# One core, RWKV-5 attention followed by a Wave-MLP block: the same tasks in another hand-written order on every engine, with other choices of engine, PSUM bank, load order and filler matmuls

## The chip, the cores and the metric

The kernel runs on one core of a Trainium2 chip. The metric is device time in microseconds (us), the median of several runs; lower is better. A core has five engines that run at the same time, each through its own list of instructions, strictly in order: PE (matrix multiply; "PEld" is its loading of weights), DVE (vector), ACT (scalar, with lookup functions), POOL (general purpose) and SP (which here only starts DMA transfers). An instruction that waits for another engine or for a transfer holds up everything behind it on its own engine. PE writes only to PSUM, of which there are eight banks; DVE and ACT read them out.

## The reference

Inputs are r, k, v of shape (4, 8, 768, 48), a decay w and a bonus u per head and channel, and four weight matrices. Two stages follow each other, the first one's output y being the second one's input x (4 x 768 x 384).

```python
for t in range(S):                       # attention, for each batch and head
    y[t] = r[t] @ (state + outer(u * k[t], v[t]))
    state = w[:, None] * state + outer(k[t], v[t])

theta = x @ w_theta                      # Wave-MLP
zr, zi = x * cos(theta), x * sin(theta)
u_ = x + w_tok_r @ zr + w_tok_i @ zi     # mixes the 768 tokens of a batch
out = u_ + relu(u_ @ w_ch)
```

## The kernel before

The recurrence is done in chunks. The work is cut into 12 groups of 256 tokens: batch b has groups 3b, 3b+1 and 3b+2. Within a group the decays are folded into r and k (tiles `Rw`, `Kw`, line 563 or 565: load times a table of powers), both are turned on PE (`flip`, L499, into PSUM) and copied out (`RT`, `KT`, L514 on ACT or L515 on DVE). PE multiplies them into scores (L606 or L619), DVE multiplies the scores by a causal mask (`mAT`, L631), and PE adds mask times v (L786, L852), states times r (L773, L827) and a diagonal bonus (L802) into a bank that becomes the attention output `x` (L810, L812, L862). The state runs from group to group: PE forms outer products of `Kw` and v (L689), DVE adds them up (`F`, `T`, L724), `N` is the decayed state that the next group starts from, and `Sb`, `Sd` are its bf16 copies. `PD` (L642) and `yd` (L668) serve the bonus. v is cast to bf16 as `vb` (L584 on ACT, L586 on DVE, L588 on POOL).

Then `x` is turned (into `xT`), PE multiplies by w_theta (L876), ACT takes cosine and sine (L883, L887), and DVE forms `z` (L891), which holds x cos and x sin. When all three groups of a batch have their z, PE mixes the tokens: 6 output tiles of 128 tokens, each in three parts of four matmuls (L912, one part for each group's z), 72 parts in all. DVE adds x (`un`, in the tile `uu_all`, L930), the result is turned (`uT`, in `uu_all` too), PE multiplies by w_ch (L944), and DVE or ACT and POOL finish the output (`fin_all`, L953, L950, L957), which SP writes out, 256 tokens at a time (L968) and for the last group 128 at a time (L963). A turn is done on PE with a copy, or by a DMA transpose that SP starts (L505); both ends are then in SBUF.

The weights come in through transfers that POOL issues (L468), land in buffers that other tiles use later (`z`, `x`, `uu_all`, `fin_all`), and are turned on PE into `WrT` and `WiT`. They may start only when k and r of group 0 have landed (the list `gate`).

`Plan.add` records 777 tasks with what each reads and writes; it works out which earlier tasks each must wait for. Nothing is scheduled by rule: six tables decide. `ORDER` is the order in which the tasks are issued, and so the order on each engine; `WAYS` picks, task by task, one of the task's possible engines; `BANKS` gives each PSUM use its bank; `AFTER` holds pairs (a, b): b also waits for a; `IDLE` holds (task, bank, n): n matmuls whose result nobody reads ("unread", from `zero`, L289) are issued right behind a task; `WARM` are 6 and 8 more such matmuls that are tasks of their own. The unread matmuls keep PE active where it would wait. The tasks below are named by what they write and the number of the group: `Kw0` in a row of the order is the buffer 0 of `Kw`.

Of the kernel before, what the change touches and what calls it, by code (L numbers as in the profile page):

```python
# [93 lines left out]
)  # L94

AFTER = [
    (84, 77), (87, 130), (170, 136), (492, 604),
]

IDLE = [  # L100
    (5, 0, 3), (30, 2, 4), (118, 5, 1), (116, 2, 2), (85, 3, 2), (88, 6, 2),
]


# [907 lines left out]
```

## Time and profile before

| | us |
|---|---|
| median of 3 runs | 140.81 (140.75 to 141.16) |
| the profiled execution, its own time | 140.54 |
| its span, from the first to the last instruction | 138.8 |
| PE busy | 127.3 (92%) |
| DVE busy | 112.2 (81%) |
| ACT busy | 79.0 (57%) |
| POOL busy | 48.9 (35%) |

The mean granted TensorE clock of the execution is 0.995. A group of instructions is named by line, engine and operation; "x8" is a count; the square bracket in a row of the timeline is how long the engine stood idle just before and whose work ended that. Matmuls overlap, so a single matmul's duration is longer than the distance to the next; the chain of waits gives the distance. The span is 1.74 us shorter than the execution's time, and the execution is 0.27 us faster than the median.

### The profile page before, as it was taken

To read this page: it belongs to the slowest core of one execution; us is meant where nothing else is said; L and a number is where in the kernel's file an instruction comes from. 1 tells how busy PE (TensorE), PEld (TensorE's weight loads), DVE (VectorE), ACT (ScalarE), POOL (GpSimd) and SP (SyncE) were. 2 spreads that over 40 slices of the span, in tenths; PEclk is the share of its full clock that TensorE was granted. 3 is DMA by queue.
4 is the path that set the end of the run, shared out by engine and by line. 5 is a ranking of instruction groups with operands and counts; after the bars stand their busy time and mean duration, and the time that the engine had idled before them with its cause. 6 is when DMAs were issued, how large, how long until landed. Compare 5 with 4: busy or idle time off the path is not lost.

```text
span 138.8 us, 5143 instructions
## 1 busy us (share of the span) xinstructions
PE 127.3 (92%) x2217; PEld 84.3 (61%) x2217; DVE 112.2 (81%) x218; ACT 79.0 (57%) x153; POOL 48.9 (35%) x57
## 2 busy tenths in 40 slices
PE   7959997989999997999999999988999999999980
PEld 2345664756678855768666676855666666655630
DVE  7599978867689999999999899994979779446480
ACT  4479897497428995899768743555910150550100
POOL 8006677490000790799000019926054311000000
PEclk9999999999999999999999999999999999999997
DMA  3999999999989980328999983999900636740545
GB/s 95 324 325 290 201 213 210 222 239 249 261 234 305 250 183 4 114 82 224 214 226 268 192 178 69 122 143 302 231 5 6 112 64 137 219 159 0 113 158 182
DMA packets 64021, 24.72 MB, mean 178 GB/s; under 512 B 58621, under 2 KB 63998, under 8 KB 63998
## 3 DMA queue, kind: packets, MB, share of 16 engines
q1 hardware_dynamic: 61520, 21.44, 65.9%
q0 software_dynamic: 2464, 2.95, 12.2%
q8 instruction: 17, 0.28, 0.9%
q14 instruction: 6, 0.05, 0.1%
q10 hardware_dynamic: 14, 0.00, 0.0%
HBM read 20.06 MB, written 4.72 MB: 179 GB/s over the span
## 4 chain that ended last, share of the span: by engine, by line
PE 66%; DVE 13%; ACT 9%; issue 5%; DMA 4%; ACTq 0%; DVEq 0%
PE bank L912 31%; PE bank L876 7%; PE bank L499 7%; PE bank L944 6%; PE bank L289 4%; DMA uu_all<-uu_all 4%; DVE mAT L631 4%; ACT KT L514 2%; PE bank L689 2%; ACT RT L514 2%; PE bank L852 2%; DVE fin_all L953 2%; PE bank L786 1%; PE bank L619 1%; PE bank L827 1%
## 5 line engine op out<-in xcount | busy, mean ns | idle before, releaser
L912 PE MATMUL bank<-z,WrT 128*128 128x384 bf16 x144 | 46.9, 326 | 0.5 <-ACT WrT L514 0.5
L912 PE MATMUL bank<-z,WiT 128*128 128x384 bf16 x144 | 46.8, 326 | 0.0
L642 POOL TENSOR_TENSOR PD<-RT,KT 128x1024 bf16<-128x1024 bf16 x4 | 8.5, 2126 | 33.6 <-ACT RT L514 31.9
L631 DVE TENSOR_TENSOR mAT<-bank,mask 128x512 bf16<-128x512 f32 x28 | 18.1, 682 | 1.4 <-PE bank L606 1.2
L912 PEld LDWEIGHTS <-WiT 128*128 128x128 bf16 x144 | 14.1, 98 | 8.4 <-issue 0.6
L912 PEld LDWEIGHTS <-WrT 128*128 128x128 bf16 x144 | 14.1, 98 | 8.4 <-DVE z L891 0.3
L887 ACT ACTIVATE trig<-bank 128x384 f16<-128x384 f32 x24 | 11.5, 494 | 11.5 <-PE bank L876 11.5
L930 DVE TENSOR_TENSOR uu_all<-bank,x 128x384 bf16<-128x384 f32 x24 | 13.1, 552 | 5.5 <-PE bank L912 5.0
L944 PE MATMUL bank<-Wch,uu_all 128*128 128x384 bf16 x72 | 15.0, 327 | 1.5 <-DMA uu_all<-uu_all 1.1
L953 DVE SCALAR_TENSOR_TENSOR fin_all<-bank,uu_all 128x384 f32<-128x384 f32 x23 | 12.1, 552 | 4.5 <-PE bank L944 4.2
L891 DVE TENSOR_TENSOR z<-x,trig 128x1536 bf16<-128x1536 bf16 x12 | 12.1, 1016 | 3.8 <-ACT trig L883 2.4
L883 ACT ACTIVATE trig<-bank,pi 128x384 f16<-128x384 f32 x24 | 13.3, 580 | 2.8 <-PE bank L876 2.8
L876 PE MATMUL bank<-Wth,xT 128*128 128x384 bf16 x72 | 14.5, 326 | 0.0
L668 POOL TENSOR_TENSOR yd<-dg,vb 128x768 bf16<-128x768 f32 x7 | 10.3, 1472 | 11.2 <-DVE z L891 5.1
L514 ACT ACTIVATE RT<-bank 128x1024 bf16<-128x1024 bf16 x12 | 12.3, 1026 | 0.3 <-PE bank L499 0.3
L514 ACT ACTIVATE KT<-bank 128x1024 bf16<-128x1024 bf16 x10 | 10.3, 1028 | 2.6 <-PE bank L499 2.6
L289 PE MATMUL bank<-zero 128*128 128x512 bf16 x28 | 8.8, 446 | 1.2 <-DVE zero L296 1.0
L944 PEld LDWEIGHTS <-uu_all 128*128 128x128 bf16 x72 | 6.2, 97 | 5.9 <-DMA uu_all<-uu_all 1.8
L563 DVE TENSOR_TENSOR Rw<-ld,rpow 128x768 bf16<-128x768 f32 x9 | 9.7, 1089 | 0.0
L499 PE MATMUL bank<-ident,Rw 128*128 128x128 bf16 x96 | 7.3, 219 | 1.7 <-DVE Rw L563 1.4
L876 PEld LDWEIGHTS <-xT 128*128 128x128 bf16 x72 | 6.5, 98 | 3.7
L499 PE MATMUL bank<-ident,Kw 128*128 128x128 bf16 x96 | 7.2, 219 | 1.4 <-DVE Kw L563 1.4
(121 smaller groups left out, 222.3 us busy)
## 6 DMA issues: line engine op xcount, KB each, us to landing
ld<-in_r_dram SPq DMA_DIRECT2D x12, 384.0 KB, 5.0
out_dram<-fin_all SPq DMA_DIRECT2D x11, 384.0 KB, 3.0
ld<-in_k_dram SPq DMA_DIRECT2D x7, 384.0 KB, 6.5
ld<-in_v_dram SPq DMA_DIRECT2D x7, 384.0 KB, 5.3
ld<-in_v_dram SPq DMA_DIRECT2D x10, 192.0 KB, 3.7
ld<-in_k_dram SPq DMA_DIRECT2D x10, 192.0 KB, 3.8
uu_all<-in_moe_w_tok_r_dram POOLq DMA_DIRECT2D x1, 384.0 KB, 7.1
z<-in_moe_w_tok_i_dram POOLq DMA_DIRECT2D x1, 384.0 KB, 8.6
```

Source lines behind the costliest of these rows:

```text
L289: ins = [nc.tensor.matmul(bank_t[k][:, :wide * C].rearrange("p (a c) -> p a c", a=wide), zero, bc(zero, 1, wide), start=True, stop=True, s ...
L499: ins = [nc.tensor.matmul(bank16(tok)[:, i * C:(i + 1) * C], s, ident, is_transpose=True, start=(i == 0), stop=(i == n - 1)) for i, s in e ...
L514: ways = [act(n * C, lambda: nc.scalar.activation(dst, src(), Act.Copy)), dve(n * C, lambda: nc.vector.tensor_copy(dst, src()), 1.0 if pai ...
L631: mask01[:, j] if pairs else mask_c): nc.vector.tensor_mul(
L876: ins = [nc.tensor.matmul(bank(th)[:, :HD], xT[:, t, dk, :], Wth[:, dk, :], start=(dk == 0), stop=(dk == ND - 1)) for dk in range(ND)]
L883: P.add(act(HD, lambda th=th, t=t, trig=trig: nc.scalar.activation(trig[:, t, 0], bank(th)[:, :HD], Act.Sin, bias=pi2), 144), use=[th], rd ...
L887: P.add(act(HD, lambda th=th, t=t, trig=trig: nc.scalar.activation(trig[:, t, 1], bank(th)[:, :HD], Act.Sin)), use=[th], rd=["sin"], wr=[( ...
L891: P.add(dve(4 * HD, lambda trig=trig, pr=pr: nc.vector.tensor_mul(z[:, 2 * pr:2 * pr + 2], bc(x[:, 2 * pr:2 * pr + 2], 2, 2), trig), 2.0, ...
L912: ins.append(nc.tensor.matmul(bank(tm)[:, :HD], (WrT, WiT)[ri][:, so, to * C:(to + 1) * C], z[:, so, ri], start=(part == 0 and i == 0), st ...
L930: P.add(dve(HD, lambda tm=tm, t=t, to=to, un=un: nc.vector.tensor_add(un[:, t], bank(tm)[:, :HD], x[:, to])), use=[tm], rd=[("x", xi, pr, ...
L944: ins = [nc.tensor.matmul(bank(tf)[:, :HD], uT[:, t, dk, :], Wch[:, dk, :], start=(dk == 0), stop=(dk == ND - 1)) for dk in range(ND)]
L953: nc.vector.scalar_tensor_tensor(fin[:, t], bank(tf)[:, :HD], 0.0, un[:, t], op0=Alu.max, op1=Alu.add))], use=[tf], rd=[("un", j, t)],
```

## The change

`ORDER`, `WAYS`, `BANKS`, `AFTER` and `IDLE` are replaced; the code is otherwise the same and computes the same values. Each engine's list is thereby another, from the first rows to the last. Over the whole program these counts change, among others: decays (`Rw`, `Kw`) on DVE 17 to 11, on POOL 7 to 13; `PD` on DVE 8 to 10, on POOL 4 to 2; `yd` on DVE 5 to 3, on POOL 7 to 9; turns of `x` by DMA 5 to 7, of `un` by DMA 8 to 7; unread matmuls 28 to 26. The first line of `ORDER` and the two short tables in the diff:

```diff
-    1, 8, 37, 0, 15, 7, 19, 5, 2, 9, 28, 36, 29, 16, 11, 112, 6, 18, 14, 12, 10, 20, 17, 21,
...
+    1, 18, 38, 2, 15, 0, 28, 5, 112, 7, 37, 19, 9, 6, 8, 16, 11, 10, 29, 20, 154, 21, 36, 77,
...
 AFTER = [
-    (84, 77), (87, 130), (170, 136), (492, 604),
+    (157, 90), (84, 158), (127, 87), (432, 434), (645, 653),
 ]
 
 IDLE = [
-    (5, 0, 3), (30, 2, 4), (118, 5, 1), (116, 2, 2), (85, 3, 2), (88, 6, 2),
+    (30, 2, 5), (118, 4, 2), (88, 7, 3), (116, 2, 1), (96, 1, 1),
 ]
```

Task 5 is the warm-up of 8 unread matmuls, task 4 the one of 6, 30 the turn of w and u ("wu flip"). Task 4 stood far behind 30, between the scores of group 1 and the outer products of group 1; it now stands right ahead of 30. Task 90 is a POOL copy of a state that now waits for `Kw` of group 2 on DVE; 158 is a POOL `Rw` that waits for `PD` on DVE; 87 is `yd` of group 0, now on POOL, waiting for `PD` of group 1; 434 is an `N` on POOL that waits for a DVE copy.

Three places of the lists follow. First DVE at the start, from the first decay on; before:

```order
L563 TENSOR_TENSOR Kw0_108<-ld0_90,kpow_81 128x8x2x48
L563 TENSOR_TENSOR Rw0_106<-ld1_91,rpow_80 128x8x2x48
L563 TENSOR_TENSOR Rw1_107<-ld4_94,rpow_80 128x8x2x48
L563 TENSOR_TENSOR Kw1_109<-ld3_93,kpow_81 128x8x2x48
L642 TENSOR_TENSOR PD0_125<-RT0_118,KT0_122 128x1024
L435 TENSOR_TENSOR uw_89<-bank1_62,wup_86 64x4 x2
L631 TENSOR_TENSOR mAT0_127<-bank6_67,mask01_72 128x512
L631 TENSOR_TENSOR mAT0_127<-bank5_66,mask01_72 128x512
L563 TENSOR_TENSOR Kw2_110<-ld6_96,kpow_81 128x8x2x48
```

and now:

```order
L563 TENSOR_TENSOR Rw0_106<-ld1_91,rpow_80 128x8x2x48
L303 MEMSET pi2_76 128x1
L563 TENSOR_TENSOR Rw1_107<-ld4_94,rpow_80 128x8x2x48
L563 TENSOR_TENSOR Kw0_108<-ld0_90,kpow_81 128x8x2x48
L563 TENSOR_TENSOR Kw1_109<-ld3_93,kpow_81 128x8x2x48
L563 TENSOR_TENSOR Kw2_110<-ld6_96,kpow_81 128x8x2x48
L420 COPY wup_86<-bank1_62 128x4
L435 TENSOR_TENSOR uw_89<-bank1_62,wup_86 64x4 x2
L724 TENSOR_TENSOR T0_136<-bank6_67,F0_131 128x192
L642 TENSOR_TENSOR PD0_125<-RT0_118,KT0_122 128x1024
L631 TENSOR_TENSOR mAT0_127<-bank0_61,mask01_72 128x512
```

All five decays come first, k's behind r's; on SP the load of k for group 0 (`ld0`) goes from second to fifth place, behind v (`ld2`), r of group 1, r of group 0 and k of group 2. Second, POOL from the `Kw` of group 3 on; before:

```order
L563 TENSOR_TENSOR Kw3_111<-ld9_99,kpow_81 128x8x2x48
L468 DMA Wch_172<-in_moe_w_ch_dram 128x3x384
L642 TENSOR_TENSOR PD0_125<-RT0_118,KT1_123 128x1024
L668 TENSOR_TENSOR yd0_157<-dg0_154,vb3_115 128x768
L752 TENSOR_TENSOR N0_134<-T1_137,w256_87 128x192
L563 TENSOR_TENSOR Rw1_107<-ld0_90,rpow_80 128x8x2x48
```

and now:

```order
L563 TENSOR_TENSOR Kw3_111<-ld9_99,kpow_81 128x8x2x48
L712 CAST Sd3_153<-N1_135 64x4x48
L468 DMA x2_162<-in_moe_w_tok_i_dram 128x2x768
L468 DMA z1_164<-in_moe_w_tok_r_dram 128x2x768
L563 TENSOR_TENSOR Kw0_108<-ld12_102,kpow_81 128x8x2x48
L468 DMA Wch_172<-in_moe_w_ch_dram 128x3x384
L563 TENSOR_TENSOR Kw2_110<-ld2_92,kpow_81 128x8x2x48
L563 TENSOR_TENSOR Rw0_106<-ld3_93,rpow_80 128x8x2x48
L712 CAST Sd1_151<-F2_133 64x4x48
L668 TENSOR_TENSOR yd0_157<-dg0_154,vb3_115 128x768
L752 TENSOR_TENSOR N0_134<-T1_137,w256_87 128x192
L565 TENSOR_TENSOR Kw3_111<-ld5_95,kpow_c_82 128x16x48
```

Between the first decay and the next `yd` there are now three more decays. Third, SP at the end, which starts the last transfers; before:

```order
L505 DMA_TRANSPOSE xT1_168<-x0_160 128x6x128
L968 DMA out_0_dram<-fin_all_169 128x2x384 x2
L505 DMA_TRANSPOSE uu_all_170<-uu_all_170 128x6x128 x2
L968 DMA out_0_dram<-fin_all_169 128x2x384 x2
L963 DMA out_0_dram<-fin_all_169 128x384 x2
```

and now:

```order
L505 DMA_TRANSPOSE xT1_168<-x0_160 128x6x128
L968 DMA out_0_dram<-fin_all_169 128x2x384
L505 DMA_TRANSPOSE uu_all_170<-uu_all_170 128x6x128
L968 DMA out_0_dram<-fin_all_169 128x2x384
L963 DMA out_0_dram<-fin_all_169 128x384 x2
L968 DMA out_0_dram<-fin_all_169 128x2x384
```

The last output is now one of 256 tokens (group 9), and one of the last two turns of `un` by DMA is gone: it stands on PE, at the end of its list.

More of the change, by code (lines that the diff above doesn't have):

```diff
@@ new lines @@
+    "000001000100000000100000000000100010000000000000000000012000000000000000010110110000"
+    "000000101101100000000001011011000011000020000000000000000100000112000000000000110000"
+    "000001002010200100000000120000000000000100000000000000100000000012000000000000000120"
+    "110110000000001201100000000000012011011000000100000001001001010000100000000120000000"
+    "000000100000010000010000000000000001200000000000011000100000000201000000000120000000"
+    "000000001201101100000000012011011000000000120110000000000000101101100000000012011011"
@@ L88 @@
+    "000000000000110000110"
 )
 BANKS = (
-    "001234567234675130425576152715460374061573605146037162051426713475123045341605273015"
-    "634562104315704367413076250376245013720167023146506560560312652405712436150274652367"
-    "5103450617406471260754161352613507413062130630714523"
+    "001123456720451670123546126452317416032413472051307510473062072307320536502615643746"
+    "172304637125036471506451726501362456731450371265140104023574602471062354731524713062"
+    "745164305721643271506153402714026174325061064327150"
```

13 lines of the change are left out of this document (3 added, 10 removed), and 82 rows, old and new, of the table ORDER.

## The prediction

> **What bounds the kernel now.** I read the page's busy shares and slices first, then a table by stretches of 10 us, then the timelines of PE, DVE and POOL where PE had gaps, and last the end of the chain of waits. The page's first part and its chain by engine:
>
> ```profile
> PE 127.3 (92%) x2217; PEld 84.3 (61%) x2217; DVE 112.2 (81%) x218; ACT 79.0 (57%) x153; POOL 48.9 (35%) x57
> PE 66%; DVE 13%; ACT 9%; issue 5%; DMA 4%; ACTq 0%; DVEq 0%
> ```
>
> PE is the bound, and a reorder does not change what PE must do; it can only change the 138.8 - 127.3 = 11.5 us in which PE stands idle. Where those lie, from the table by stretches (us; busy time of PE, PEld, DVE, ACT, POOL; clock; DMA):
>
> ```profile
> 20.00:30.00 10.00, 8.82 (x201) 6.31 (x199) 7.63 (x15) 7.29 (x16) 7.21 (x9) 1.00 1.17 213
> 50.00:60.00 10.00, 8.81 (x216) 6.10 (x215) 10.00 (x17) 7.75 (x16) 5.35 (x5) 1.00 0.28 80
> 90.00:100.00 10.00, 8.95 (x102) 5.43 (x100) 7.50 (x16) 7.03 (x16) 3.49 (x4) 1.00 1.11 227
> 130.00:138.80 8.80, 4.66 (x32) 2.53 (x30) 3.86 (x8) 0.49 (x1) 0.00 (x0) 0.91 0.48 155
> ```
>
> The reader is to see four places: the lead-in until the mixing of batch 0 begins, 50 to 60 (PE 1.2 idle, and DVE never idle), 90 to 100 (1.05), and the end (4.1). They hold 7.5 of the 11.5 us. PE at the lead-in and at the first mixing matmul:
>
> ```profile
> 8.15 0.61 PE L499 MATMUL bank<-ident,Kw 128*128 128x128 bf16 x8 [1.20 <-DVE Kw L563]
> ...
> 16.24 1.46 PE L289 MATMUL bank<-zero 128*128 128x512 bf16 x6 [0.23 <-DVE mAT L631]
> ...
> 31.23 0.32 PE L912 MATMUL bank<-z,WrT 128*128 128x384 bf16 x1 [0.52 <-ACT WrT L514]
> ```
>
> Mixing begins at 31.23, when the first z is done. From there on PE mostly has mixing to fill in with; so what the lead-in gains or loses goes through to the end, unless PE starves later.
>
> **The lead-in.** DVE's timeline gives its waits up to the first z:
>
> ```profile
> 7.05 0.96 DVE L563 TENSOR_TENSOR Kw<-ld,kpow 128x768 bf16<-128x768 f32 x1 [0.86 <-ACT kpow L400]
> ...
> 18.12 0.36 DVE L724 TENSOR_TENSOR F<-bank,N 128x192 f32<-128x192 f32 x1 [0.74 <-PE bank L689]
> ...
> 24.67 0.69 DVE L631 TENSOR_TENSOR mAT<-bank,mask 128x512 bf16<-128x512 f32 x1 [1.00 <-PE bank L606]
> ...
> 28.99 0.56 DVE L812 CAST x<-bank 128x384 bf16<-128x384 f32 x1 [1.32 <-PE bank L802]
> 29.47 1.71 DVE L891 TENSOR_TENSOR z<-x,trig 128x1536 bf16<-128x1536 bf16 x1
> ```
>
> From 7.05 to 29.47 DVE waits 0.74 + 1.00 + 1.32 = 3.06 us in three places and otherwise works. Its new list up to the first z has the same five decays, twelve mask products, three PD and one yd; some items have changed places with others of like size; what comes on top is the small mask and `wup`, for which I put 0.4. So the first z moves by what happens to the waits.
>
> The 0.74 is made by PE: the six unread matmuls at 16.24 take 1.46 and the outer products (L689), for which DVE waits, stand behind them. The change puts those six ahead of the turn of w and u, at a time when PE waits for its first decay anyway (1.20 at 8.15). I count -0.74. The 1.32 is a wait for the bonus of group 2, to copy its x; that copy now stands behind the first z: -1.32. The 1.00 is a wait for scores of group 2, where PE itself stood; I find nothing in the lists that ends it: 0 (bound -1.00).
>
> Against that, the load of k for group 0 goes from second to fifth. SP's fifth row, and the page's row on the loads of r (size, median us from issue to landing):
>
> ```profile
> 4.24 1.20 SPq L446 DMA_DIRECT2D ld<-in_v_dram  x1
> ```
>
> ```profile
> ld<-in_r_dram SPq DMA_DIRECT2D x12, 384.0 KB, 5.0
> ```
>
> The fifth load is issued at 4.24 and would land near 4.24 + 5.0 = 9.2. DVE does two r decays first (from about 7.0, 0.95 each): free at 8.9, so +0.3. In all the first z comes 0.74 + 1.32 - 0.4 - 0.3 = 1.36 earlier (bounds: 0.7 later if no wait goes, 2.4 earlier if all go).
>
> PE has also done more by then. Distances from the chain of waits:
>
> ```profile
> 72.34 0.47 PE bank L499 x8
> 72.81 0.49 PE bank L876 x3
> 73.30 0.65 PE bank L912 x4
> ```
>
> A turn of eight blocks costs 0.47 and so one of six 0.35, a product with w_theta or (of the same shape) w_ch 0.49, a part of mixing 0.65. Ahead of the first mixing part PE's new list has one turn of eight and two of weights more and one turn of x less: 0.47 + 0.35 = 0.8 of work that before came later. It is free because PE waits for z there. Lead-in: -1.36 - 0.8 = -2.16. Bounds: -0.1 (no wait goes, +0.7 and -0.8) to -3.2.
>
> **The added waits.** On POOL, a state's copy waits for `Kw` of group 2 on DVE (9.2 + 3 x 0.95 = 12.1), and the `Rw` of group 2 for the PD behind that (about 13.5). Behind them on POOL are two issues of weights, N and `yd` of group 0; DVE's next F waits for that N: 13.5 + 1.8 + 0.5 = 15.8. That F has four mask products of 0.69 and a PD ahead of it on DVE, so it comes at 13.5 + 2.8 = 16.3 or later: 0. If the cover fails, it costs up to the decay's 1.8; that belongs to POOL's rival below.
>
> **PE's own work.** Two turns of x go to DMA and one of `un` comes back, 6 blocks less: -0.35. The two unread matmuls less lie where PE waits: 0.
>
> **50 to 60.** DVE's and POOL's rows here, and PE's:
>
> ```profile
> 28.53 1.82 POOL L563 TENSOR_TENSOR Kw<-ld,kpow 128x768 bf16<-128x768 f32 x1
> ...
> 50.06 1.82 POOL L563 TENSOR_TENSOR Rw<-ld,rpow 128x768 bf16<-128x768 f32 x1
> ```
>
> ```profile
> 50.50 2.20 DVE L563 TENSOR_TENSOR Rw<-ld,rpow 128x768 bf16<-128x768 f32 x1
> ```
>
> ```profile
> 52.75 0.62 PE L499 MATMUL bank<-ident,Rw 128*128 128x128 bf16 x8 [0.93 <-DVE Rw L563]
> ```
>
> DVE's decay began during POOL's and ended 0.82 after it (52.70 against 51.88), as if it had begun only when POOL was done; the k decay at 7.05, of the same shape, took 0.96. PE waited 0.93 for it. The first z above met the POOL `Kw` of 28.53 in the same way: it ended at 31.18, 0.83 after that `Kw`. This `Rw`, of group 6, is among the decays that move to POOL (`Rw0<-ld3` in the second order above): -0.93 if it is there in time. It then stands right behind another decay on POOL, 1.82; if PE waits for that instead, +0.9. I take -0.45, half of the gain.
>
> The Trainium skill, page "SBUF — State Buffer", section "Who interferes with whom", says that a DVE instruction with two SBUF inputs contends with a POOL instruction that reads SBUF, and that the loser is blocked for the whole of the other; the rows above agree (2.20 for 0.96). By that rule six more POOL decays, each met halfway through by such a DVE instruction, would put 6 x 0.91 = 5.5 us of blocking on DVE, an estimate, and if PE waited for all of it the sum would be +3.4 and not -2.1.
>
> **Turns by DMA.** Thirteen become fourteen. PE waits for two of them:
>
> ```profile
> 90.83 0.66 PE L944 MATMUL bank<-Wch,uu_all 128*128 128x384 bf16 x3 [0.34 <-DMA uu_all<-uu_all]
> ...
> 94.24 0.66 PE L944 MATMUL bank<-Wch,uu_all 128*128 128x384 bf16 x3 [0.71 <-DMA uu_all<-uu_all]
> ```
>
> On SP they stand among loads, which wait behind a turn that is not ready. In the new list the three turns of `un` of batch 1 are together, and the products that need them come later on PE. 0, bounds -1.05 and +1.05.
>
> **The end.** PE's last steps, and DVE's, from the chain of waits; the product at 132.37 follows the last part of mixing:
>
> ```profile
> 132.37 0.50 PE bank L944 x3
> ...
> 134.26 0.41 PE bank L944 x2
> 134.66 0.35 issue
> 135.01 0.56 DVE fin_all L953
> ```
>
> Outputs leave in two sizes (size, median us to landing):
>
> ```profile
> out_dram<-fin_all SPq DMA_DIRECT2D x11, 384.0 KB, 3.0
> ```
>
> ```profile
> out_dram<-fin_all SPq DMA_DIRECT2D x2, 192.0 KB, 1.9
> ```
>
> Before, behind the last part of mixing (132.37) stand four products and half a turn: 4 x 0.49 + 0.18 = 2.1. DVE ends at 135.57, and the span, with the last transfer of 192 KB, at 138.8: 3.2 later. Now six products, two half turns and one whole turn follow: 2.94 + 0.36 + 0.35 = 3.6, so the last part of mixing ends 1.5 earlier, at 130.9. The last product starts 3.6 - 0.5 = 3.1 behind it, DVE begins 0.75 after that (135.01 against 134.26) and takes 0.56: 4.4. The last transfer is now one of 384 KB, 1.1 more to landing: 4.3. 130.9 + 4.4 + 4.3 = 139.6 against 138.8: +0.85 (0.2 if the size of the last transfer costs little, 1.2 if the whole turn waits for DVE).
>
> **The sum.** -2.16 - 0.35 - 0.45 + 0.85 = -2.1 on the profiled execution's 140.54 (span 138.8 and 1.7 around it): 138.4. That execution is 0.27 under the median of 140.81, so the median after is 138.7.
>
> **The rivals.** POOL becomes the bound (slower). The six decays cost POOL 6 x 1.82 = 10.9 us, and the second order above has four decays almost in a row, where one stood before, at a time when DVE makes the three z of batch 0 and decays, all with two SBUF inputs. Each collision costs PE 0.93 by the row at 52.75. Two are paid by the gain (1.9 of 2.1); from the third on the sum is positive: three give 138.7 + 2.8 = 141.5, four 142.4. For it: the two collisions seen in 48.9 us of POOL. Against it: the pairs in `AFTER` keep some apart, and not every DVE wait reaches PE. 141.5 to 142.4, chance 0.24.
>
> The lead is lost to transfers (no change). The page's GB/s by slices of 3.47 us:
>
> ```profile
> GB/s 95 324 325 290 201 213 210 222 239 249 261 234 305 250 183 4 114 82 224 214 226 268 192 178 69 122 143 302 231 5 6 112 64 137 219 159 0 113 158 182
> ```
>
> Loads alone move at 324; from the fourth slice on, with weights, at about 210. POOL now issues the first weights as soon as k and r of group 0 have landed, near 9.2, while before that stood behind a cast of v. Loads of groups 2 to 4 are then slower, and a decay that waits for one holds up DVE or POOL. If that eats the lead-in's 2.16, 138.7 + 2.16 = 140.9. For it: the fifth of nine loads is issued at 4.24 and takes 1.20 to issue, so they are not through before 10. Against: POOL's list spaces the later weights by decays. Chance 0.18.
>
> More goes than I count: the 1.00 of the lead-in and the 1.05 of the DMA turns: 138.7 - 2.05 = 136.7. Chance 0.13. The forecast itself has 0.45.
>
> **How the numbers follow.** About 0.3% (0.4 us) is what a measurement of this kernel can tell from no change. Under 140.4 are nearly all of the forecast's case (0.43), the case of more (0.13), a third of the lost lead (0.06) and a little of POOL's (0.03): faster 0.65. Within: 0.02 + 0.07 + 0.01 = 0.10. Slower: the rest, 0.25. The forecast's own range is 137.4 to 140.2 (the lead-in's bounds are -1.0 and +2.1 from its value, the other terms' smaller and unlikely to fall together). The range over the cases goes from 136.7 to 142.2, which leaves out half of the best case and a third of POOL's.
>
> **What would show it.** Right: the first mixing matmul near 30 with a turn of `Kw` and eight turns of weights ahead of it; no unread matmuls between 15 and 18; no DVE decay of 2.2 near 50; PE busy 126 to 127 in a span of 136 to 137; the last DVE instruction 4.4 behind the last L912, and over 4 us from there to the end. Wrong: several DVE rows of L563, L642 or L891 twice their usual length with PE waits on them (POOL); waits of DVE or POOL for `ld` between 15 and 40 (transfers); or a first mixing matmul at 31 or later.

## The result, and the profile after

| | before | after |
|---|---|---|
| median of 4 runs, us | 140.96 (140.75 to 141.16) | 147.29 (145.21 to 149.47) |
| ratio to before, 95% interval | | 1.036 (1.025 to 1.047) |
| the profiled execution, us | 140.54 | 149.47 |
| its span, us | 138.8 | 147.7 |
| its mean TensorE clock | 0.995 | 0.954 |
| first mixing matmul (L912), us | 31.23 | 38.22 |

The changed kernel is slower by 3.6%; 138.7 was forecast, with a range to 142.2. Here and below the medians are over all executions, while the ratios leave out executions over 1.5% above the fastest of their kernel, so the two can differ (by the medians after is 4.5% slower). The profiled execution of after is the longest of its four.

The page of after, its busy shares, the clock and GB/s by slices of 3.69 us, and the chain by engine:

```profile
PE 131.6 (89%) x2209; PEld 87.2 (59%) x2209; DVE 115.7 (78%) x212; ACT 76.8 (52%) x145; POOL 61.1 (41%) x70
...
PEclk9996899559999999999999997799999999999999
...
GB/s 118 275 296 284 304 260 248 232 221 203 235 242 141 4 0 50 283 190 254 36 250 205 167 188 39 96 116 274 233 209 115 63 58 107 277 102 0 53 146 174
...
PE 61%; DVE 14%; DMA 12%; SPq 4%; ACT 3%; issue 2%; DVEq 0%; ACTq 0%
```

PE has fewer instructions than before (2209 for 2217) and is busy 4.3 us longer: its clock fell to half in parts of the first 35 us, and again between 90 and 94. Transfers now hold 12% of the chain, before 4%. The stretches of 10 us at the start (PE, PEld, DVE, ACT, POOL busy; clock; DMA):

```profile
10.00:20.00 10.00, 8.40 (x188) 5.63 (x189) 8.57 (x17) 6.93 (x12) 4.04 (x6) 0.83 1.11 283
20.00:30.00 10.00, 5.90 (x129) 4.27 (x128) 9.14 (x11) 4.60 (x10) 9.65 (x10) 0.80 1.18 250
30.00:40.00 10.00, 10.00 (x163) 7.63 (x162) 9.18 (x16) 7.78 (x16) 1.21 (x3) 0.86 1.14 222
```

PE is idle 5.7 us between 10 and 30, and the clock is at 0.80 to 0.86 up to 40. Of the 8.9 us that the span is longer, 7.0 are there when mixing begins. PE's two long waits on the way, and the first mixing matmul (the row at 10.53 names DVE's little memset of `pi` between two decays; what PE turns there is the first decay):

```profile
10.53 0.61 PE L499 MATMUL bank<-ident,Rw 128*128 128x128 bf16 x8 [1.79 <-DVE pi L303]
...
27.39 0.74 PE L773 MATMUL bank<-Sd,RT 128*128 128x96 bf16 x7 [4.01 <-DVE mAT L631]
...
38.22 0.33 PE L912 MATMUL bank<-z,WrT 128*128 128x384 bf16 x1
```

What PE waited for, on DVE:

```profile
9.43 1.84 DVE L563 TENSOR_TENSOR Rw<-ld,rpow 128x768 bf16<-128x768 f32 x2 [3.08 <-DMA ld<-in_r_dram]
...
11.71 0.96 DVE L563 TENSOR_TENSOR Kw<-ld,kpow 128x768 bf16<-128x768 f32 x1 [0.44 <-DMA ld<-in_k_dram]
...
16.82 2.48 DVE L631 TENSOR_TENSOR mAT<-bank,mask 128x512 bf16<-128x512 f32 x4 [0.74 <-PE bank L606]
...
22.42 4.32 DVE L753 TENSOR_TENSOR N<-T,w 128x192 f32<-128x192 f32 x1
```

The first decay waits 3.08 for r of group 0. The first mask product is at 16.82 (before 11.74). And the small N of group 1, which the change moved from POOL to DVE (that of group 0 went the other way), takes 4.32, where group 0's took 0.35 on DVE before. POOL's rows bear on both:

```profile
2.58 0.89 POOL L468 DMA_DIRECT2D uu_all<-in_moe_w_tok_r_dram  x1
...
22.50 1.49 POOL L668 TENSOR_TENSOR yd<-dg,vb 128x768 bf16<-128x768 f32 x1
23.92 0.76 POOL L468 DMA_DIRECT2D fin_all<-in_moe_w_tok_i_dram  x1
24.70 1.81 POOL L563 TENSOR_TENSOR Kw<-ld,kpow 128x768 bf16<-128x768 f32 x1
```

The first weights are issued at 2.58, with no wait in front, and not near 9.2. N ended at 26.74, 0.23 behind POOL's Kw (26.51), as if it had been held up by three POOL instructions in a row. What the early weights do to the loads, from the DMA view between 3 and 12 us (packets, MB, time as a share of 16 engines; queue q1 has the loads, q0 the weights):

```profile
DMA packets 6013, 2.56 MB, mean 284 GB/s; under 512 B 5757, under 2 KB 6013, under 8 KB 6013
...
q1 hardware_dynamic: 5717, 2.16, 88.3%
q0 software_dynamic: 272, 0.39, 24.6%
```

Only 0.39 MB of weights moved, but the loads got 2.16 MB; with the weights held back (the first experiment) they get 2.90 in the same 9 us. The whole rate fell from 323 to 284 GB/s as well.

### The profile page after: what moved, and what is told of

It is laid out like the page before. It is cut to its first block, busy times and chain, and to the rows that moved or that the text cites. A ratio compares the mean times of both kernels' runs of the same rounds, so it can differ in the third digit from the quotient of the medians.

```text
span 147.7 us, 5132 instructions
## 1 busy us (share of the span) xinstructions
PE 131.6 (89%) x2209; PEld 87.2 (59%) x2209; DVE 115.7 (78%) x212; ACT 76.8 (52%) x145; POOL 61.1 (41%) x70
## 4 chain that ended last, share of the span: by engine, by line
PE 61%; DVE 14%; DMA 12%; SPq 4%; ACT 3%; issue 2%; DVEq 0%; ACTq 0%
PE bank L912 26%; PE bank L499 11%; PE bank L944 7%; PE bank L876 6%; DMA ld<-in_k_dram 5%; DVE mAT L631 4%; DVE PD L642 4%; DMA ld<-in_v_dram 4%; DMA uu_all<-uu_all 3%; DVE N L753 3%; SPq L446 3%; PE bank L606 3%; PE bank L689 2%; DVE uu_all L930 1%; PE bank L786 1%
## 5 line engine op out<-in xcount | busy, mean ns | idle before, releaser
L912 PE MATMUL bank<-z,WrT 128*128 128x384 bf16 x144 | 47.4, 330 | 0.0
L912 PE MATMUL bank<-z,WiT 128*128 128x384 bf16 x144 | 47.4, 330 | 0.0
L912 PEld LDWEIGHTS <-WrT 128*128 128x128 bf16 x144 | 14.2, 98 | 8.5 <-issue 0.2
L912 PEld LDWEIGHTS <-WiT 128*128 128x128 bf16 x144 | 14.2, 99 | 8.2 <-issue 0.2
L891 DVE TENSOR_TENSOR z<-x,trig 128x1536 bf16<-128x1536 bf16 x12 | 11.5, 957 | 6.4 <-ACT trig L887 6.1
L514 ACT ACTIVATE KT<-bank 128x1024 bf16<-128x1024 bf16 x11 | 11.2, 1021 | 9.9 <-PE bank L499 9.9
L668 POOL TENSOR_TENSOR yd<-dg,vb 128x768 bf16<-128x768 f32 x9 | 13.3, 1473 | 6.0 <-ACT dg L664 5.1
L944 PE MATMUL bank<-Wch,uu_all 128*128 128x384 bf16 x72 | 14.0, 326 | 1.8 <-DMA uu_all<-uu_all 0.7
L563 POOL TENSOR_TENSOR Rw<-ld,rpow 128x768 bf16<-128x768 f32 x7 | 13.7, 1962 | 4.5 <-PE bank L499 4.4
L514 ACT ACTIVATE RT<-bank 128x1024 bf16<-128x1024 bf16 x10 | 10.2, 1023 | 3.9 <-PE bank L499 3.9
L642 DVE TENSOR_TENSOR PD<-RT,KT 128x1024 bf16<-128x1024 bf16 x10 | 9.9, 996 | 2.4 <-ACT RT L514 1.6
L584 ACT ACTIVATE vb<-ld 128x768 bf16<-128x768 f32 x10 | 8.4, 839 | 2.2 <-DMA ld<-in_v_dram 2.2
L563 POOL TENSOR_TENSOR Kw<-ld,kpow 128x768 bf16<-128x768 f32 x3 | 5.8, 1942 | 8.8 <-DMA ld<-in_k_dram 8.8
```

The source lines that it names most:

```text
L514: ways = [act(n * C, lambda: nc.scalar.activation(dst, src(), Act.Copy)), dve(n * C, lambda: nc.vector.tensor_copy(dst, src()), 1.0 if pai ...
L563: return eng.tensor_mul(to.rearrange("p j h d -> p h j d")[:, :, :, :D], tokens(i), pw)
L642: return eng.tensor_mul(flat[2], flat[0], flat[1])
L668: return eng.tensor_mul(yd.rearrange("p a b d -> p (a b) d"), wide(dg, D), vb.rearrange("p a b d -> p (a b) d"))
L912: ins.append(nc.tensor.matmul(bank(tm)[:, :HD], (WrT, WiT)[ri][:, so, to * C:(to + 1) * C], z[:, so, ri], start=(part == 0 and i == 0), st ...
L944: ins = [nc.tensor.matmul(bank(tf)[:, :HD], uT[:, t, dk, :], Wch[:, dk, :], start=(dk == 0), stop=(dk == ND - 1)) for dk in range(ND)]
```

## The experiments

All ratios are to the kernel before, run beside them on the same chip. "First mixing" is the first L912 on PE in the kernel's one trace. It is no measure of the time: e8 begins mixing at 31.10 and is 5.7% slower than before, e12 at 32.04 and is 1% faster. It also differs by chance between traces: in before, e12, e14, e15 and e16, whose DVE has the same list up to there, the first decay starts at 7.05, 8.20, 6.78, 6.97 and 8.56.

| run | kernel | median, us (executions) | ratio (95%) | first mixing |
|---|---|---|---|---|
| e1_weights_wait | new, weights wait for k of group 0 | 142.72 (10) | 1.003 (0.997 to 1.010) | 31.64 |
| e2_n1_pool | new, N of group 1 on POOL | 144.75 (4) | 1.018 (1.011 to 1.025) | 34.90 |
| e3_both | both | 143.62 (7) | 1.012 (1.006 to 1.018) | 30.99 |
| e4_before_early | before, first weights early | 140.74 (10) | 0.998 (0.994 to 1.003) | 32.27 |
| e5_before_no_idle | before, without IDLE | 140.94 (10) | 1.003 (0.998 to 1.007) | 32.18 |
| e6_loads | new, k of group 0 loaded third | 146.91 (4) | not given | 38.03 |
| e7_loads_wait | new, that and weights held | 142.41 (10) | 1.005 (0.999 to 1.011) | 31.05 |
| e8_engines | new, weights held, old engines | 148.30 (4) | 1.057 (1.048 to 1.067) | 31.10 |
| e9_x | e7 and N on POOL | 144.67 (4) | 1.019 (1.009 to 1.029) | 31.60 |
| e10_apart | e9 and two pairs for PD | 142.03 (10) | 0.998 (0.993 to 1.003) | 30.35 |
| e11_tail | e9 with the end of before | 142.52 (10) | 1.000 (0.995 to 1.005) | 30.26 |
| e12_before_two | before, two waits removed | 139.58 (12) | 0.990 (0.986 to 0.994) | 32.04 |
| e13_apart4 | e10 and two pairs for decays | 141.86 (12) | 1.001 (0.995 to 1.007) | 30.28 |
| e14_before_warm | before, one unread for six | 139.97 (12) | 0.993 (0.989 to 0.998) | 30.07 |
| e15_before_pair | before, one pair | 139.15 (6) | 0.989 (0.983 to 0.994) | 31.11 |
| e16_before_three | before, both and one pair more | 139.02 (6) | 0.985 (0.979 to 0.992) | 31.73 |
| e17_hold | e13 and five unread | 140.97 (12) | 0.991 (0.986 to 0.995) | 30.36 |
| e18_products | e13, six products reordered | 140.43 (12) | 0.993 (0.989 to 0.998) | 30.14 |

Before had medians of 140.7 (e1 to e4), 140.6 (e5 to e8), 140.8 (e9 to e12), 141.4 (e13 to e16) and 141.1 (e17, e18).

### The early weights and N

The theory was that weights that start at 2.6 starve the loads; the rivals were the block of N by POOL, and the lower clock. First the weights (task 36 is the load of k of group 0, 50 the first weights):

```diff
-    (157, 90), (84, 158), (127, 87), (432, 434), (645, 653),
+    (157, 90), (84, 158), (127, 87), (432, 434), (645, 653), (36, 50),
```

> The changed kernel with one more pair, (36, 50): the first transfer of weights waits until k of group 0 has landed, as the prediction took it to do. If the early weights, which start at 2.6 and share the DMA engines with the first loads, are what costs most: the loads come 1.2 apart again, k of group 0 lands near 9.2, DVE's first decay starts near 7.5 and not at 9.43, the first mixing matmul comes at 34 to 35 and not at 38.2, and the time falls from 147.3 to 143 to 144. If the stall of N on DVE behind POOL is the main cause and the transfers are hidden anyway: the first mixing matmul stays above 37 and the time above 146. If only the lower clock of PE costs: no more than 1 us either way.

The ratio falls from 1.036 to 1.003 (that of the medians from 1.045 to 1.014), and mixing begins at 31.64: more than was expected of it, since N's stall goes too. POOL and DVE in its trace:

```profile
9.41 0.89 POOL L468 DMA_DIRECT2D uu_all<-in_moe_w_tok_r_dram  x1 [6.78 <-DMA ld<-in_k_dram]
```

```profile
6.82 1.84 DVE L563 TENSOR_TENSOR Rw<-ld,rpow 128x768 bf16<-128x768 f32 x2 [0.39 <-DMA ld<-in_r_dram]
...
9.20 0.96 DVE L563 TENSOR_TENSOR Kw<-ld,kpow 128x768 bf16<-128x768 f32 x1 [0.55 <-DMA ld<-in_k_dram]
...
13.52 2.48 DVE L631 TENSOR_TENSOR mAT<-bank,mask 128x512 bf16<-128x512 f32 x4
...
20.19 0.35 DVE L753 TENSOR_TENSOR N<-T,w 128x192 f32<-128x192 f32 x1
```

The first mask product is 3.3 earlier (13.52 for 16.82), and N takes 0.35 although it is still on DVE: moved by some 2 to 3 us, it no longer meets POOL's yd and Kw in the same way. The 3.3 and the 4.0 of PE's wait behind N are 7.3, of which 6.6 show where mixing begins. DMA between 3 and 12 us, for the numbers used above:

```profile
DMA packets 7690, 2.90 MB, mean 323 GB/s; under 512 B 7690, under 2 KB 7690, under 8 KB 7690
```

N alone, put on POOL ahead of yd of group 1 by its digit in `WAYS` (the rows as they leave DVE and come to POOL), and then both edits:

```diff
-L753 TENSOR_TENSOR N_135<-T_136,w_87 128x192
+L752 TENSOR_TENSOR N_135<-T_136,w_87 128x192
 L668 TENSOR_TENSOR yd_158<-dg_155,vb_113 128x768
```

> The changed kernel with N of group 1 on POOL again, ahead of yd of group 1, so that DVE has no N of 4.32 at 22.4. If that stall is the main cause: PE's wait of 4.01 at 27.4 goes, the first mixing matmul comes at 34 to 35 and not at 38.2, and the time falls from 147.3 to 143 to 144. If the early weights are the main cause and the N only used up time for which DVE would have waited elsewhere: first mixing at 37 or later, time above 146. If the locks are everywhere (each POOL decay against some DVE instruction with two inputs), another instruction of DVE takes over the stall, 2 us or more, and the time stays above 146 too, but with that row to be seen.

> The changed kernel with both edits: the first weights wait for k of group 0, and N of group 1 is on POOL. If these two are the whole loss of the lead-in and add up: first mixing near 31, as before, PE's clock near 1.0 in all of 10 to 35, and a time of 139.5 to 141.5. If the two cover for each other (one wait takes the place of the other), first mixing stays at 33 or later and the time at 143 or more. If the lower clock is a cause of its own, the clock stays at 0.8 between 10 and 30 although the waits are gone.

N alone: 1.018, half of the loss, with mixing 3.3 earlier. So with early weights about half of the loss comes through N (the ratios of e2 and of after rest on two executions each; by the medians it is a third). The two do not add up: both edits give 1.012, and no less than the weights alone, though mixing begins at 30.99. In e2 a cast on DVE meets POOL in N's place (a cast of this size took 0.40 in before):

```profile
24.13 2.40 DVE L713 CAST Sd<-N 64x192 bf16<-64x192 f32 x1
```

Then the same early weights in the kernel before, moved on POOL from behind the cast of v to ahead of it:

```diff
+L468 DMA uu_all<-in_moe_w_tok_r_dram 128x2x768
 L588 CAST vb_112<-ld_92 128x768
-L468 DMA uu_all<-in_moe_w_tok_r_dram 128x2x768
```

> The kernel before, with nothing changed but the place of the first transfer of weights on POOL: right behind the zeros of Rw and ahead of the cast of v, so that it starts near 3 and not at 12.3. If early weights starve the loads in any order: loads 1.2 to 1.6 apart from the third on, first mixing 2 to 3.5 later than 31.2, time 143 to 144.5. If the old order of the loads (k and r of group 0 first) keeps the first decays out of it: first mixing at 31.2 to 32.2, time 141 to 142.

They cost nothing there: 0.998. POOL issues them at 3.37, and DVE's first decays wait for no load:

```profile
7.75 0.96 DVE L563 TENSOR_TENSOR Kw<-ld,kpow 128x768 bf16<-128x768 f32 x1 [0.88 <-ACT kpow L400]
8.69 1.83 DVE L563 TENSOR_TENSOR Rw<-ld,rpow 128x768 bf16<-128x768 f32 x2
10.43 0.95 DVE L563 TENSOR_TENSOR Kw<-ld,kpow 128x768 bf16<-128x768 f32 x1
```

The loads lose about as much as in after (before, they get 2.91 MB between 3 and 12 us):

```profile
q1 hardware_dynamic: 5973, 2.26, 91.1%
```

So neither the early weights nor the new order of DVE and loads costs much by itself; together they cost 3.3%. What in the new order makes it vulnerable was tried next: k of group 0 third among the loads (v0, r0, k0, r1, k1, k2), with early weights and with weights held until k of group 2 has landed ((154, 50) in `AFTER`). SP's rows:

```diff
 L446 DMA ld_92<-in_v_dram 128x8x96
-L446 DMA ld_94<-in_r_dram 128x8x96
 L446 DMA ld_91<-in_r_dram 128x8x96
-L446 DMA ld_96<-in_k_dram 128x8x96
 L446 DMA ld_90<-in_k_dram 128x8x96
+L446 DMA ld_94<-in_r_dram 128x8x96
 L446 DMA ld_93<-in_k_dram 128x8x96
+L446 DMA ld_96<-in_k_dram 128x8x96
```

> The changed kernel with k of group 0 third among the loads and not fifth (v0, r0, k0, r1, k1, k2), the weights still starting at 2.6. If the loss is early weights and a late k0 together: k0 lands near 7.8 and not at 10.5, DVE's Kw0 ends 1 to 1.5 earlier, first mixing 1 to 3 earlier than 38.2, time 144.5 to 146. If the place of k0 is all: first mixing below 33 and a time of 142 to 143.5. If N's stall of 4.3 on DVE decides in any case: first mixing above 37, time above 146.

> The same order of loads, and the first weights wait for k of group 2, the sixth load (near 9.8): both causes of the late start undone. If k0's place still costs 0.5 to 1 with the weights held (Kw0 started at 9.20 in the kernel that holds the weights only): first mixing 0.5 to 1 earlier than its 31.6, time 0.5 to 1 below its 142.7. If DVE's start is bound by the r's and by its own five decays: no difference from 142.7 within 0.5.

Not the place of k0: with early weights nothing is gained (146.9), since DVE now waits for the next load, and N is blocked as before:

```profile
10.32 0.96 DVE L563 TENSOR_TENSOR Rw<-ld,rpow 128x768 bf16<-128x768 f32 x1 [2.25 <-DMA ld<-in_r_dram]
...
22.22 4.33 DVE L753 TENSOR_TENSOR N<-T,w 128x192 f32<-128x192 f32 x1
```

That leaves the five decays at the head of DVE's list, which want five loads one behind the other, in whatever order these come; no run moves them, so this is argued and not shown. With the weights held, 1.005 against 1.003: k0's place is worth nothing that can be told, though mixing begins 0.6 earlier.

### The clock

The kernel before without the table `IDLE`, so that PE pauses more at the start:

```diff
-    (5, 0, 3), (30, 2, 4), (118, 5, 1), (116, 2, 2), (85, 3, 2), (88, 6, 2),
```

> The kernel before without the 14 unread matmuls of IDLE (the warm-ups of 8 and 6 stay). If PE's clock falls by itself as soon as PE pauses near the start, so that the pauses of the changed kernel cost twice: a clock of 0.5 to 0.8 somewhere between 10 and 30, first mixing 0.5 to 2 later than 31.2, and 141.5 to 143. If the clock needs a pause of over 1 us, which these gaps are not: clock near 1.0 throughout and a time within 0.5 of 140.7.

```profile
PEclk9968599999999999999999999999999999999998
```

The clock falls, to half in the slice from 13.9 to 17.3, and mixing begins 0.95 later; but the ratio is 1.003 (0.998 to 1.007). A lower clock of this size at the start is no cause of 3.6%. In after the clock falls for longer (PE busy 131.6 us, here 126.8); what that adds to its loss is not shown apart from the waits.

### POOL's larger share

The rival with the highest chance: POOL has more to do and blocks DVE. The changed kernel, weights held, with the old engine for 53 tasks (`WAYS` of before at their places; some of the digits):

```diff
-WAYS[87], WAYS[93], WAYS[136], WAYS[238], WAYS[370], WAYS[371], ... = 0, 0, 1, 1, 1, 1, ...
+WAYS[87], WAYS[93], WAYS[136], WAYS[238], WAYS[370], WAYS[371], ... = 1, 1, 0, 0, 0, 0, ...
```

> The changed kernel with the weights held until k of group 0 has landed, and with the choice of engine of the kernel before for all 53 tasks of DVE, ACT and POOL that had another one (decays, PD, yd, N, copies of states, copies of x, casts of v; not the turns and the last step of the output). The order of all tasks is as in the changed kernel. If POOL's share (13 decays, the blocking of DVE) is what is left of the loss: DVE's rows of 2.2 and more go, and the time falls from 142.7 to 140.7 or below. If the order is what is left: 142 or more. If the old engines do not fit the new order (DVE has more to do and becomes late): above 143.

1.057: the old engines do not fit the new order (whose pairs in `AFTER` stay). Mixing begins at 31.1 as with the new ones; the loss comes after. In this trace too DVE stands behind POOL, through three instructions:

```profile
61.59 3.80 DVE L642 TENSOR_TENSOR PD<-RT,KT 128x1024 bf16<-128x1024 bf16 x1
```

```profile
60.20 2.12 POOL L642 TENSOR_TENSOR PD<-RT,KT 128x1024 bf16<-128x1024 bf16 x1
62.26 0.82 POOL L588 CAST vb<-ld 128x768 bf16<-128x768 f32 x1
63.05 1.80 POOL L563 TENSOR_TENSOR Rw<-ld,rpow 128x768 bf16<-128x768 f32 x1
```

Meetings like these do not need a larger share of POOL: 51.2 us of POOL here, 61.1 in after. This run changes 53 choices at once, so it does not say what each is worth; but less work on POOL did not mean less loss.

### What is left: meetings, the end, the turns by DMA

With the weights held the changed kernel was about level with before (1.4% above it by the medians of e1), not the forecast 1.5% faster. e9 has the loads of e7, the weights held and N on POOL. e10 adds two pairs, e13 two more, that make POOL wait for DVE; e11 is e9 with the last 54 tasks as in before (order, engines and banks).

```diff
 AFTER = [  # e9, e11; then e10; then e13
-    (157, 90), (84, 158), (127, 87), (432, 434), (645, 653),
+    (157, 90), (84, 158), (127, 87), (432, 434), (645, 653), (154, 50),
+    (466, 549), (294, 415),
+    (239, 370), (281, 371),
```

> The changed kernel with three edits: the order of loads v0, r0, k0, r1, k1, k2, the first weights held until k2 has landed, and N of group 1 on POOL. If the start is then as the prediction took it to be: first mixing at 29.5 to 30.5, no N of 1.9 and more on DVE, and a time of 139.5 to 141.5. If what is left of the loss (142.4 against 140.6 with the first two edits alone) has nothing to do with that N: 142 to 143 again, and single executions that differ by up to 5 us.

> The same kernel with two more pairs, which keep POOL from reading while DVE makes PD: the POOL k decay of group 9 waits for PD of group 8, the POOL r decay of group 7 for PD of group 5. If blocking of DVE by POOL is what is left of the loss and of the spread: no PD above 1 us, PE's waits for PD near 60 and 80 go, 1 to 2 us less than the kernel without the pairs, and a smaller spread. If it is not: no difference beyond 0.5.

> The changed kernel with the three edits, the two pairs of PD, and two pairs more: the POOL k decay of group 6 waits for the DVE r decay of group 4 (they started 0.04 apart at 37.6 in a long execution, the DVE one then took 2.58), and the POOL r decay of group 6 for the DVE k decay of group 5 (2.57 in every trace). If these meetings are what makes single executions differ by 5 us: hardly any execution above 142, a median of 139.5 to 140.5, at or below the kernel before. If not: a median near 142 and executions up to 145 as without the pairs, with no DVE decay above 1 us in the trace. If the later POOL decays are waited for: above 143.

e9 is the slowest of these, by four executions. Its trace shows a meeting of decays that start 0.04 apart, POOL's first; DVE's then takes 2.58 and not 0.95:

```profile
37.67 2.58 DVE L563 TENSOR_TENSOR Rw<-ld,rpow 128x768 bf16<-128x768 f32 x1
```

```profile
37.63 1.80 POOL L563 TENSOR_TENSOR Kw<-ld,kpow 128x768 bf16<-128x768 f32 x1 [1.07 <-DMA ld<-in_k_dram]
```

With the two pairs for PD the ratio is 0.998, for 1.019 in e9. But e11, which lacks them, has 1.000, and in its trace PD, 0.68 by itself, is held up twice:

```profile
57.78 2.90 DVE L642 TENSOR_TENSOR PD<-RT,KT 128x1024 bf16<-128x1024 bf16 x2
...
79.20 2.15 DVE L642 TENSOR_TENSOR PD<-RT,KT 128x1024 bf16<-128x1024 bf16 x1 [0.91 <-ACT KT L514]
```

So what the pairs are worth is not shown, and e9's 1.019 stays unexplained. The two pairs for decays bring nothing more: 1.001, although no DVE decay in e13's trace is above 1 us; so the theory that such meetings make up the rest fell there. The pairs also move meetings rather than end them: in the trace of e17 (below), which has all four, a POOL decay of another group is met, in an execution of only 139.88 us:

```profile
36.42 2.57 DVE L563 TENSOR_TENSOR Rw<-ld,rpow 128x768 bf16<-128x768 f32 x1
```

Executions of e13 still range from 139.9 to 144.5; this wide range of the new order is not explained here.

> The changed kernel with the first three edits, and the end of the kernel before: the last 54 tasks (mixing of batch 3 and all behind it) in the order, with the engines and banks of before; the last output is again one of 128 tokens. If the prediction's term for the end (+0.85) holds: 0.85 less than the kernel without this edit, the last mixing matmul about 1.5 later and the end 2.3 less behind it. If the shorter last transfer and the PE work behind the last mixing cancel: within 0.3 of it.

The end: the product behind the last part of mixing starts at 134.65 in e11 and at 139.71 in after, where DVE's last steps end at 144.06:

```profile
134.65 1.14 PE L944 MATMUL bank<-Wch,uu_all 128*128 128x384 bf16 x6
```

```profile
139.71 0.65 PE L944 MATMUL bank<-Wch,uu_all 128*128 128x384 bf16 x3
```

```profile
142.04 2.02 DVE L953 SCALAR_TENSOR_TENSOR fin_all<-bank,uu_all 128x384 f32<-128x384 f32 x4
```

From there to the end (141.0 and 147.7) it is 6.4 in e11 (6.4 to 6.6 in before, by the chain and by the timeline) and 8.0 in after. That is some 1.5 more, and 1.5 us of PE work that now stands there was ahead of it before: the two cancel. The times do not settle it: e11's ratio is 0.019 below that of e9, the kernel that it was made from, far more than 0.85 us, but e10 lies as low without this edit, and e9 rests on few executions.

In the traces of e1, e3, e7, e10 and e13 the longest wait of PE behind the lead-in is for a turn of `un` by DMA (1.14 to 1.55); in e13:

```profile
86.95 4.78 PE L944 MATMUL bank<-Wch,uu_all 128*128 128x384 bf16 x18 [1.54 <-DMA uu_all<-uu_all]
```

Six products stand together, in the order of the groups 5, 3, 4, while SP starts the turns in the order 4, 5, 3. e17 puts five unread matmuls in front (`(405, 5, 5)` in `IDLE`), e18 puts the products, and what follows from them, in the order 4, 5, 3 (tasks by number: first of each product pair):

```diff
 IDLE = [  # e17
-    (30, 2, 5), (118, 4, 2), (88, 7, 3), (116, 2, 1), (96, 1, 1),
+    (30, 2, 5), (118, 4, 2), (88, 7, 3), (116, 2, 1), (96, 1, 1), (405, 5, 5),
 PE's products in ORDER  # e18
-    537, 540, 506, 503, 520, 523
+    520, 523, 540, 537, 503, 506
```

> The changed kernel with three edits and four pairs, and five unread matmuls (about 1.1 us) behind the product with w_theta after which PE waits 1.54 for a turn by DMA at 85 to 87. If PE's clock, which fell to 0.72 in 85 to 90 behind that wait (18 products took 4.78 and not 3.10), makes the long executions: hardly any above 142, a median 0.7 to 1.5 below the kernel without them (141.9). If the wait itself is the loss and the clock hardly matters: within 0.4 of 141.9. If the spread comes from elsewhere: executions up to 144.5 as before.

> The changed kernel with three edits and four pairs, and the six products behind that wait in the order in which their turns by DMA end: group 4, 5, 3 and not 5, 3, 4. If PE waits there only because the product of the second turn stands first: the wait falls from 1.54 to below 0.8, the clock stays, and the time falls by 0.7 to 2 below 141.9. If the three turns by DMA land together, so that the order tells nothing: no difference, and then the turns by DMA themselves are what PE waits for.

The ratios are 0.991 and 0.993, against 1.001 in e13; the interval of e18 still overlaps that of e13, and the medians give 0.999 and 0.995 against 1.003. In e18 PE waits 0.37 for the last turn instead of 1.54 (and 1.08 later for a turn of x); in e17 the wait is filled and the 18 products take 3.10, not 4.78, at full clock:

```profile
85.15 2.11 PE L944 MATMUL bank<-Wch,uu_all 128*128 128x384 bf16 x12
87.63 1.15 PE L944 MATMUL bank<-Wch,uu_all 128*128 128x384 bf16 x6 [0.37 <-DMA uu_all<-uu_all]
```

```profile
86.84 1.24 PE L289 MATMUL bank<-zero 128*128 128x512 bf16 x5
88.22 3.10 PE L944 MATMUL bank<-Wch,uu_all 128*128 128x384 bf16 x18
```

So the turns by DMA, which the forecast put at zero, cost the new order some 0.4 to 1.0% by these figures, and in e13's trace part of that is the clock behind the wait. Executions of both range over 4 to 6 us still.

### The gains that were forecast, by themselves

In the kernel before: one unread matmul for six at 16.24 (e14), a pair (282 also moves behind 371 in `ORDER`, which leaves every engine's own list as it was) that lets the POOL decay of group 5 wait for the DVE decay of group 6 (e15), both (e12), and both with a pair that lets POOL's Kw of group 3 wait for the first z (e16).

```diff
-WARM, WARM_NS = [6, 8], [1280, 1700]
+WARM, WARM_NS = [1, 8], [1280, 1700]
-    (84, 77), (87, 130), (170, 136), (492, 604),
+    (84, 77), (87, 130), (170, 136), (492, 604), (371, 282), (110, 195),
```

> The kernel before with one unread matmul in place of six at 16.2, nothing else. If the prediction's 0.74 was right: DVE's wait at 18.1 goes and the time is 0.5 to 0.8 less than before. If what follows waits for something else: within 0.3 of before. If PE's clock falls without them: 0.3 or more above it.

> The kernel before with the pair that keeps the POOL r decay of group 5 behind the DVE r decay of group 6, nothing else. If the prediction's 0.93 goes through to the end: 0.6 to 0.95 less than before. If PE finds its next wait behind it: within 0.3. Together with the kernel with one unread matmul it should give the 1.0 per cent that both edits gave, if they add up.

> The kernel before with two waits taken away that the prediction counted as gains: one unread matmul in place of six at 16.2 (DVE's wait of 0.74 at 18.1), and the POOL r decay of group 5 waits for the DVE r decay of group 6, so that DVE is not blocked at 50.5 (2.20 for 0.96, PE waits 0.93). If both terms were sized rightly and go through to the end: first mixing 0.7 earlier, 1.2 to 1.7 less in all, 139.1 to 139.5. If DVE or PE waits for the next thing instead: 140.3 to 140.9. If the later r decay on POOL is waited for: 141 or more.

> The kernel before with the two edits, and the POOL k decay of group 3 waits for the first z on DVE, which POOL blocked (2.01 for 0.95). If that block reaches PE (first mixing waits for z, 0.81): first mixing about 0.8 earlier and 0.5 to 0.8 less than the 139.6 with two edits, 138.8 to 139.1. If the mixing then waits for the turned weights or PE for the later decay: 139.4 or more.

Both gains are clear of noise: 0.7% (0.2 to 1.2) for the unread matmuls, where 0.74 us are 0.5%, and 1.15% (0.6 to 1.7) for the pair, where 0.93 us are 0.7%. Together they give 1.0% (0.6 to 1.4), below the sum of 1.85%; e12 ran on another chip, so whether they add up stays open. Mixing came later in e12's trace than was expected, at 32.04, because its first decay came 1.15 later than in before; counted from that decay, mixing begins 24.2 behind it in before and 24.1 in e15, 23.3 in e14, 23.8 in e12 and 23.2 in e16. In e15 DVE's decay takes 0.95 and POOL's follows:

```profile
50.37 0.95 DVE L563 TENSOR_TENSOR Rw<-ld,rpow 128x768 bf16<-128x768 f32 x1
```

```profile
51.45 1.82 POOL L563 TENSOR_TENSOR Rw<-ld,rpow 128x768 bf16<-128x768 f32 x1 [1.48 <-PE bank L689]
```

e16 has the lowest ratio of all kernels here, 0.985 (0.979 to 0.992), 139.02 us against 141.38, though its interval overlaps those of its neighbours. So two pairs and one digit in the kernel before give at least as much as the new order in its best form here (e17, 0.991). Its first z takes 0.96 and POOL's Kw starts behind it:

```profile
30.62 0.96 DVE L891 TENSOR_TENSOR z<-x,trig 128x1536 bf16<-128x1536 bf16 x1
```

```profile
31.67 1.81 POOL L563 TENSOR_TENSOR Kw<-ld,kpow 128x768 bf16<-128x768 f32 x1 [2.01 <-DVE z L891]
```

## Why the prediction was wrong

**The step that failed** is one half-sentence under the rivals: "POOL now issues the first weights as soon as k and r of group 0 have landed, near 9.2". They are issued at 2.58. The list `gate` (the description of the kernel above shares the error) makes the weights stand behind those two loads in `ORDER`, and only that: no instruction waits on it. POOL's rows of before:

```profile
11.53 0.82 POOL L588 CAST vb<-ld 128x768 bf16<-128x768 f32 x1 [8.09 <-DVE PD L642]
12.29 0.74 POOL L468 DMA_DIRECT2D uu_all<-in_moe_w_tok_r_dram  x1
```

The issue at 12.29 came from POOL's list alone, where a cast that a pair in `AFTER` held stood ahead. The change moved that cast to DVE, and the hold went with it. The order's rows could have told this, since nothing that waits stands ahead of the weights in POOL's new list; the trace of before could not, because there the wait was the cast's. In the sum, the step is the lead-in's term of +0.3: DVE was to begin its first decay at about 7.0 and the k decay of group 0 at 9.2. They began at 9.43 and 11.71; with the one wait put in (e1) they begin at 6.82 and 9.20, and 3.3 of the 3.6% are gone.

**The rival with transfers** (0.18) named the mechanism and half of its place, "loads of groups 2 to 4 are then slower". Its price was bounded by the lead-in's gain of 2.16, which no row supported. Measured: the first mask product 3.3 later, and behind it N. Its row of GB/s was read one slice early: the fourth slice has 290, and near 210 it is from the fifth on.

**Blocking** was priced at 0.93 a meeting, from the one that the trace of before showed. N's cost PE 4.0, as DVE was held, by the rows, through three POOL instructions in a row. That about half of the loss comes through N (1.018 without it) was in no case of the forecast; nor that it vanishes when the start moves by 3 us. POOL's rival as it was put, six decays more as such, has no support: the old engines in the new order make 1.057. The Trainium skill, page "SBUF — State Buffer", section "Who interferes with whom", has the loser blocked for the whole of the other instruction; the 4.32 for 0.35 agrees as to the sign and is longer than any one POOL instruction there (1.81).

**The lead-in**, -2.16: with the weights held, mixing begins at 31.64, 31.05 or 30.3 (e1, e7, e13), so between +0.4 and -0.9. Nor does what the lead-in gains go through to the end, as the prediction had it: e3 and e13 begin mixing before 31.23 and are no faster than before (1.012 and 1.001), e4 begins 1.04 later and is no slower (0.998). The wait of 0.74 for the unread matmuls goes as forecast and is worth that much (e14). What failed is that DVE's items had "changed places with others of like size": N of group 1 for that of group 0 is such a change, and with five decays first, the first mask product comes at 13.52, and not 11.74, even with the weights held. I had +0.3 for that.

**50 to 60**: the DVE decay of 2.20 near 50 is gone and PE does not wait between 50 and 60, as forecast. But another decay, at 47.14, takes its place in after:

```profile
47.14 2.57 DVE L563 TENSOR_TENSOR Kw<-ld,kpow 128x768 bf16<-128x768 f32 x1
```

PE had mixing to do there and did not wait for it. The price of the old meeting was right or low (0.93 us, 0.7%; e15 has 0.6 to 1.7%).

**Turns by DMA**, 0 with bounds of 1.05: "the products that need them come later on PE" was wrong in the outcome; PE takes them in another order than the turns are started, and waits 0.73 in after and up to 1.55 in the variants. e18 puts the price at 0.7 to 0.8% (1.0 to 1.1 us), about the bound of 1.05.

**The end**, +0.85: from the last mixing part 8.0 instead of the forecast 8.7, since the last DVE instruction (144.06) is 3.6 before the end, not 4.3; the larger last transfer costs 0.4 more than the smaller one (3.2), not 1.1. With 1.5 us of work moved there the term is near 0.

**PE's busy time**, 126 to 127 forecast, is 131.6. A change of clock was in no term.

## What to carry to other kernels

A start time that one reads off a trace belongs to whatever stood ahead in the queue; when a change takes that away, ask which wait the instruction has of its own, and if it has none, take it to start at once. A transfer that comes early is priced at the loads that the critical engine waits for in that window: the same early weights cost 0 in one order and 3.3% in the other. And where DVE and POOL work side by side, one pair that lets POOL go second at a place where PE waits was worth 1% here, as much as or more than the new order of everything once its faults were mended (0.991 and 0.993, by the medians 0.999 and 0.995).

## What was not expected of the hardware

A DVE instruction with two SBUF inputs can lose to several POOL instructions in a row, 4.32 us for 0.35 (yd, a DMA issue, Kw) and 3.80 for 0.68 (PD, a cast, Rw). In these traces a hair decides whether it does: by the rows, which are rough on POOL, N began 0.08 ahead of yd in after and was held, and 0.10 ahead in e1 (20.19, yd at 20.29) and was not.

A transfer of weights (1536 B a packet in q0) took 0.39 MB while the loads beside it (384 B) lost 0.74 MB, and the sum fell from 323 to 284 GB/s.

PE's clock fell to half behind a wait of 1.54 in e13, so that 18 products took 4.78 and not 3.10; behind 1.55 in e10 it did not. The Trainium skill, page "TensorE: Matmul & The Clock Gate", section "Why this matters for your kernels", asks for no idle gaps of PE over about 3 us; here half of that was enough in one execution and not in another.
